# A convolution followed by a feed-forward layer on one core: GpSimd's additions one step later and spread out

## The chip, the core and the metric

The kernel runs on one core of a Trainium2 chip. The metric is the device time of one execution in microseconds (us). TensorE (PE in the profile) multiplies matrices, VectorE (DVE) and ScalarE (ACT) work element by element, GpSimd (POOL) does that too and issues some DMAs, and SyncE (SP) issues the other DMAs. PEld is the loading of a matmul's stationary operand, which overlaps with the matmul before it.

## The reference

The input x has 8 x 4096 tokens of 192 channels. First comes a causal convolution over 7 tokens, with weights that are shared by groups of 24 channels; then a feed-forward layer of width 2048 with a piecewise activation.

```python
w = softmax(weight, axis=-1)                      # 8 groups x 7 taps
y[t, c] = sum(w[c // 24, k] * x[t - 6 + k, c] for k in range(7))
h = y @ w_in                                      # 192 -> 2048
g = np.where(h >= 1, h, np.where(h <= -1, 0, (h + 1) ** 2 / 4))
out = g @ w_out                                   # 2048 -> 192
```

## The kernel before, in words

The 32768 tokens are worked through in 64 blocks of 512; two blocks make a chunk. A **step** q is one pair of 128-wide slices of the 2048 hidden units for one block, so a block has 8 steps, a chunk 16 (i = 0 to 15 in the code, blocks 0 to 7 and 8 to 15), and the kernel 512. Everything is written in one order by hand; each engine keeps that order.

float32 products are made from rounded parts: x is held as `hi` and `lo`, the activations as `gh` and `gl`. Of 192 channels, the first 128 stand in a "natural" and in a "swapped" copy (lower and upper 64 partitions exchanged), so that two 64-row matmuls run beside each other. One step on TensorE is 18 such pairs: `mm1(q)` (L475) takes the natural `hi, hi, lo`, the swapped `hi, hi, lo` and the remaining channels `rhi, rhi, rlo` in this order, then `mm2(q - 3)` (L528) nine pairs of gh, gl and of the sum of low parts, `m`.

In the code's step q ScalarE squares the activation of h(q) (L562, L563) and rounds g(q - 1) to `gh` (L573); VectorE makes `gl` (L579, `act_low(q - 1)`), their sum `m` over the two slices (L585, `act_sum(q - 1)`) and the activation's last part (L890, `act_most(q)`). h has two buffers in PSUM, so `mm1(q + 2)` waits for L890 of q. ScalarE starts on h(q) when `mm1(q)` is done; so what stands in the code's step i behind it runs while TensorE is in step i + 1. A **TensorE step** below counts by `mm1`.

Between this, the convolution of the next blocks is made: units `a` and `b` for the two blocks' natural channels, `r` for the remaining channels of both. `conv_slot(i, ...)` deals out its operations by tables (`PLAN_A`, `PLAN_B`, `PLAN_R`): "T" is a transpose on VectorE (L163), a number is a tap. Taps of `a` are made on VectorE (L232). Of `b` and `r`, ScalarE makes a product into a buffer `p` (L237), and GpSimd adds it to `y` or `r` (L129). "split" makes `hi` on ScalarE (L268) and `lo = y - hi` on GpSimd (L272), and SP issues two transfers of 64 partitions (L255, L256) that make the swapped copy of each. Unit `b` of a chunk has its transpose and first taps at i = 12, 14 and 15 of the chunk before, the others and its split (i = 5) in its own chunk; its block starts at i = 8. The split of `a` stands at i = 12, for a block that starts at i = 0 of the next chunk.

From chunk 2 on, additions are not issued at once but kept in `held`, and `add_held` issues them behind that step's `act_sum` (each waits for the sum `m` by a dependency named "port"). The subtraction for `lo` is not held. GpSimd also issues four adding DMAs for a block's output (L619).

Of the kernel before, what the change touches and what calls it, by code (L numbers as in the profile page):

```python
# [8 lines left out]
F32 = mybir.dt.float32  # L9
# [22 lines left out]
def lightconv_then_ffn(ctx: ExitStack, tc: tile.TileContext, x, weight, w_in, w_out, out):  # L32
# [24 lines left out]
    nc = tc.nc  # L57
# [63 lines left out]

    pending = []

    held = []

    def add_held(behind):

        for out, a, b in held:
            add = nc.gpsimd.tensor_add(out, a, b)  # L129
            if behind is not None:  # L130
                tc.add_manual_dep(add.ins, behind.ins.name, mybir.DependencyInfo(
                    mybir.DependencyClass.Sync, mybir.DependencyReason.DATA), reason="port")
        held.clear()

    def let_go():

# [10 lines left out]
    class Conv:  # L147
# [92 lines left out]
        def taps(self, *ks):  # L240
            y = self.y
            for k in ks:
                if k == 0:
                    nc.scalar.mul(y, self.xT[:, SH:SH + TB], wk[:, self.wsel, 0:1])  # L244
                elif self.c == 1 and self.u != "b":
                    pending.append((y, y, self.product(k)))
                elif self.c > 1:
                    held.append((y, y, self.product(k)))
                else:
                    nc.gpsimd.tensor_add(y, y, self.product(k))  # L250

# [4 lines left out]
            nc.sync.dma_start(out=w[BOT].bitcast(F32), in_=t[TOP].bitcast(F32))  # L256
            return w

        def split(self, eng=None):
            for _ in self.splits(eng or nc.gpsimd):  # L260
                pass

        def splits(self, eng):

            o = xop[2 * self.c + (self.u == "b")]
            hi = xo.tile([P, TB], F32R, name="hi0")
            lo = xo.tile([P, TB], F32R, name="lo0")
            nc.scalar.copy(hi, self.y)  # L268
            for key, t in (("hi", hi), ("lo", lo)):
                if key == "lo":  # L270
                    yield
                    eng.tensor_sub(lo, self.y, hi.bitcast(F32))  # L272
                w = self.swapped(t, key + "1", 3)
                o["n", key] = (t[TOP], t[BOT])
                o["s", key] = (w[TOP], w[BOT])
            yield

        def split_rest(self):

# [520 lines left out]
    def whole(j, *cols):  # L800
        for _ in chunks[j].bits(*cols):
# [25 lines left out]

    PLAN_B = {12: ("T",), 14: (0, 1), 15: (2, 3), 1: (4,), 2: (5,), 3: (6,), 5: "split"}  # L830
    PLAN_A = {1: ("T",), 2: (0,), 4: (1,), 6: (2,), 7: (3,), 9: (4,), 10: (5,), 11: (6,),
              12: "split"}
    PLAN_R = {2: ("T",), 4: (0,), 6: (1,), 7: (2,), 8: (3, 4), 9: (5,), 11: (6,), 13: "split"}
    SECOND_B = {0: (0, 1), 1: (2,), 2: (3,), 3: (4,), 4: (5, 6), 5: "split"}


# [5 lines left out]
    def conv_slot(i, b, a, r):  # L842
        early = b is not None and b.c == 0
        plans = ((None if early else b, SECOND_B if b and b.c == 1 else PLAN_B),
                 (a, FIRST_A if early else PLAN_A),
                 (r, FIRST_R if early else PLAN_R))
        for u, plan in plans:
# [119 lines left out]
    for q in range(NQ + LATE):  # L967
# [16 lines left out]
        done = q - (DELAY if q < NF32 + DELAY else LATE)  # L984
        if done < 0 or q == NF32 + DELAY:
            done = None
# [27 lines left out]
        else:  # L1014
# [17 lines left out]
            if q < NQ:  # L1032
                conv_slot(i, conv_b if i < 8 else conv_n.get("b"), conv_n.get("a"),
                          conv_n.get("r"))
            add_held(act_sum(n) if low else None)
            if q == NQ - 1:
                act_low(q - 1)
# [50 lines left out]
```

## Time and profile before

| what | value |
|---|---|
| median of 3 runs | 2046.57 us (2046.46 to 2049.79) |
| the profiled execution | 2046.76 us |
| its span in the profile | 2045.0 us |
| PE, DVE, ACT, POOL busy | 100%, 96%, 96%, 39% |

The span runs from the first to the last instruction of the profiled execution; 1.8 us of its time lie outside. A busy PE counts pipelined matmuls, so that short waits of its loads hardly show in the busy share.

### The profile page before, as it was taken

What the parts mean: (1) busy time and instruction counts of PE and PEld (TensorE: products, weight loads), DVE (VectorE), ACT (ScalarE), POOL (GpSimd) and SP (SyncE); (2) the same over time, 40 slices, a digit from 0 to 9 for tenths busy, and PEclk for the clock granted to TensorE, in tenths of its full rate; (3) what the DMA queues carried; (4) which work ended last, traced back from release to release, by engine and by line L of the source; (5) the groups of instructions that cost most, each with busy time, mean ns of one, the idle gap of its engine ahead of it and who ended that gap; (6) DMA issues with size and microseconds to landing.
All of it is one profiled execution on the core that took longest, in us unless ns stands there. A gap on an engine that the chain in (4) does not pass through costs nothing.

```text
span 2045.0 us, 46902 instructions
## 1 busy us (share of the span) xinstructions
PE 2037.9 (100%) x18644; PEld 1756.9 (86%) x18644; DVE 1966.2 (96%) x2109; ACT 1960.4 (96%) x2381; POOL 792.8 (39%) x749
## 2 busy tenths in 40 slices
PE   9999999999999999999999999999999999999999
PEld 6998888888888888888888888888888888888888
DVE  8899999999999999999999999999999999999998
ACT  8799999999999999999999999999999999999997
POOL 1544343343433443334434344343343333443431
PEclk9999999999999999999999999999999999999999
DMA  7333333443434434334333344343343433433323
GB/s 178 80 62 70 69 71 71 85 76 56 81 68 79 80 65 77 71 67 87 70 66 73 72 82 76 57 83 69 74 81 65 76 71 66 86 72 65 72 55 55
DMA packets 470685, 152.27 MB, mean 74 GB/s; under 512 B 418944, under 2 KB 426624, under 8 KB 470464
## 3 DMA queue, kind: packets, MB, share of 16 engines
q1 hardware_dynamic: 446880, 109.17, 25.4%
q0 software_dynamic: 23424, 39.99, 13.4%
q8 instruction: 146, 2.39, 0.5%
q14 instruction: 75, 0.61, 0.1%
q10 hardware_dynamic: 160, 0.10, 0.0%
HBM read 32.84 MB, written 25.17 MB: 28 GB/s over the span
## 4 chain that ended last, share of the span: by engine, by line
PE 68%; DVE 15%; ACT 13%; issue 4%; DVEq 0%; ACTq 0%; POOL 0%; POOLq 0%
PE h L475 35%; PE accr L528 20%; PE accm L528 10%; DVE gl L579 7%; DVE g L890 4%; ACT gh L573 3%; ACT g L562 3%; ACT g L563 3%; DVE m L585 3%; ACT p L237 3%; DVE osb L631 1%; PE accm L495 1%; PE accr L495 1%; ACT t L609 0%; ACT y L244 0%
## 5 line engine op out<-in xcount | busy, mean ns | idle before, releaser
L579 DVE TENSOR_TENSOR gl<-g,gh 128x1024 fp32r<-128x1024 f32 x495 | 728.1, 1471 | 23.4 <-ACT gh L573 17.1
L890 DVE SCALAR_TENSOR_TENSOR g<-g,h 128x1024 f32<-128x1024 f32 x504 | 607.5, 1206 | 4.8 <-ACT g L563 2.8
L475 PE MATMUL h<-hi,w 64*128 64x512 f32 x4032 | 609.4, 380 | 1.5
L528 PE MATMUL accr<-gh,wg 64*128 64x512 f32 x3960 | 590.1, 376 | 0.0
L562 ACT ACTIVATE g<-h 128x1024 f32<-128x1024 f32 (+1 forms) x497 | 507.2, 1020 | 41.6 <-PE h L475 39.9
L563 ACT ACTIVATE g<-g 128x1024 f32<-128x1024 f32 (+1 forms) x497 | 526.6, 1060 | 15.8
L573 ACT CAST gh<-g 128x1024 fp32r<-128x1024 f32 x495 | 514.4, 1039 | 0.5 <-DVE g L890 0.4
L129 POOL TENSOR_TENSOR y<-y,p 128x512 f32<-128x512 f32 x180 | 231.0, 1283 | 573.3 <-ACT p L237 300.5
L475 PEld LDWEIGHTS h<-hi,w 64*128 64x128 f32 x4032 | 376.0, 186 | 76.4 <-DVE g L890 28.2
L528 PEld LDWEIGHTS accr<-gh,wg 64*128 64x128 f32 x3960 | 373.9, 185 | 53.2
L129 POOL TENSOR_TENSOR r<-r,p 128x512 f32<-128x512 f32 x180 | 232.5, 1291 | 476.6 <-DVE m L585 420.0
L475 PE MATMUL h<-lo,w 64*128 64x512 f32 x2016 | 383.8, 376 | 0.0
L528 PE MATMUL accr<-gl,words 64*128 64x512 f32 x1980 | 376.3, 376 | 0.0
L585 DVE TENSOR_TENSOR m<-gl 128x512 fp32r<-128x512 f32 x495 | 348.0, 703 | 20.6 <-PE h L475 0.5
L528 PE MATMUL accm<-gh,wg 64*128 64x512 f32 x1980 | 295.1, 376 | 0.0
L475 PE MATMUL h<-rh,w 64*128 64x512 f32 x992 | 293.6, 376 | 0.0
L475 PE MATMUL h<-rhi,w 64*128 64x512 f32 x992 | 293.6, 376 | 0.0
L619 POOL DMA_DIRECT2D t<-t x244 | 206.0, 983 | 97.6 <-DMA t<-t 75.6
L475 PEld LDWEIGHTS h<-lo,w 64*128 64x128 f32 x2016 | 192.2, 186 | 25.9
L528 PEld LDWEIGHTS accr<-gl,words 64*128 64x128 f32 x1980 | 188.3, 186 | 26.0
L528 PEld LDWEIGHTS accm<-gh,wg 64*128 64x128 f32 x1980 | 188.0, 186 | 26.0
L475 PEld LDWEIGHTS h<-rhi,w 64*128 64x128 f32 x992 | 184.5, 186 | 12.9
(161 smaller groups left out, 2313.3 us busy)
## 6 DMA issues: line engine op xcount, KB each, us to landing
t<-t POOLq DMA_DIRECT2D x183, 128.0 KB, 4.1
out_dram<-osb SPq DMA_DIRECT2D x366, 64.0 KB, 1.9
raw<-in_x_dram SPq DMA_DIRECT2D x334, 68.0 KB, 2.6
hi<-hi SPq DMA_DIRECT2D x128, 128.0 KB, 3.4
lo<-lo SPq DMA_DIRECT2D x126, 128.0 KB, 3.1
t<-t POOLq DMA_DIRECT2D x61, 256.0 KB, 3.3
rhi<-rh SPq DMA_DIRECT2D x62, 128.0 KB, 4.1
rlo<-rl SPq DMA_DIRECT2D x62, 128.0 KB, 3.5
```

What stands on the lines that cost most here:

```text
L129: add = nc.gpsimd.tensor_add(out, a, b)
L237: nc.scalar.mul(p, self.xT[:, SH + k:SH + k + TB], wk[:, self.wsel, k:k + 1])
L475: nc.tensor.matmul(h[e], w[HALVES[e], c0:c0 + P], seen(x[e][e]), start=(n == 0), stop=(n == len(mms) - 1))
L495: nc.tensor.matmul(accs[s][a, i][:, c0:c0 + D], block, w[half, e, :], start=(j == 0 and e == 0 and b % 2 == 0), stop=(j == NPAIR - 1 and e ...
L528: mm = nc.tensor.matmul(accs[s][bank], w[half], in_turn(g[half]), start=(j == 0 and bank not in seen), stop=(j == NPAIR - 1 and k % 3 == 2 ...
L562: nc.scalar.activation(g[:, e, :], hs[q][:, e, :], AF.Relu, bias=0.5, scale=0.5)
L563: nc.scalar.activation(g[:, e, :], g[:, e, :], AF.Square)
L573: nc.scalar.copy(gh[:, e, :], gs[q][:, e, :])
L579: nc.vector.tensor_sub(gl[:, e, :], g[:, e, :], gh[:, e, :])
L585: return nc.vector.tensor_add(gt, gl[:, 0, :], gl[:, 1, :])
L619: nc.gpsimd.dma_start(out=to, in_=src, accum_op=ALU.add)
L890: nc.vector.scalar_tensor_tensor(out=g, in0=g, scalar=1.0, in1=h, op0=ALU.min, op1=ALU.max)
```

## The change: what it does

`held` now takes functions, and there is a second list, `fresh`. What `conv_slot` puts in goes to `fresh`; `add_held` issues what is in `held`, behind the step's `act_sum` as before, and then moves `fresh` to `held`. So each addition comes one step later than before. The subtraction for `lo` with its two transfers, of `a` and `b` from chunk 2 on, goes the same way: one step later, and behind the sum of low parts. Two table entries with two taps are spread (`b`: taps 2, 3 at i = 15 become 2 at 15 and 3 at 0; `r`: taps 3, 4 at i = 8 become 3 at 8 and 4 at 9).

```diff
-        for out, a, b in held:
-            add = nc.gpsimd.tensor_add(out, a, b)
+        for work in held:
+            done = work()
             if behind is not None:
-                tc.add_manual_dep(add.ins, behind.ins.name, mybir.DependencyInfo(
+                tc.add_manual_dep(done.ins, behind.ins.name, mybir.DependencyInfo(
                     mybir.DependencyClass.Sync, mybir.DependencyReason.DATA), reason="port")
-        held.clear()
+        held[:] = fresh
+        fresh.clear()
...
                 elif self.c > 1:
-                    held.append((y, y, self.product(k)))
+                    fresh.append(lambda p=self.product(k): nc.gpsimd.tensor_add(y, y, p))
...
-        def split(self, eng=None):
-            for _ in self.splits(eng or nc.gpsimd):
-                pass
+        def split(self):
+
+            if self.c < 2:
+                for _ in self.splits(nc.gpsimd):
+                    pass
+                return
+            parts = self.splits(nc.gpsimd)
+            next(parts)
+            fresh.append(lambda: next(parts))
...
                 if key == "lo":
                     yield
-                    eng.tensor_sub(lo, self.y, hi.bitcast(F32))
+                    sub = eng.tensor_sub(lo, self.y, hi.bitcast(F32))
...
-    PLAN_B = {12: ("T",), 14: (0, 1), 15: (2, 3), 1: (4,), 2: (5,), 3: (6,), 5: "split"}
+    PLAN_B = {12: ("T",), 14: (0, 1), 15: (2,), 0: (3,), 1: (4,), 2: (5,), 3: (6,), 5: "split"}
...
-    PLAN_R = {2: ("T",), 4: (0,), 6: (1,), 7: (2,), 8: (3, 4), 9: (5,), 11: (6,), 13: "split"}
+    PLAN_R = {2: ("T",), 4: (0,), 6: (1,), 7: (2,), 8: (3,), 9: (4,), 10: (5,), 11: (6,),
+              13: "split"}
```

On GpSimd, from the additions of unit `b` to its split and the first addition of `r`, with what each row waits for (DVE is the wait behind the sum, DMASW and DMAHW are transfers). Before:

```order
L129 TENSOR_TENSOR y<-y,p 128x512 [waits DVE_49,Activation_49,Pool_49] x3
L619 DMA t<-t 128x512 [waits DMASW3_49,DMASW2_49]
L619 DMA t<-t 64x512 [waits DMASW5_49]
L619 DMA t<-t 64x512 [waits DMASW4_49]
L619 DMA t<-t 64x512
L272 TENSOR_TENSOR lo_4261<-y,hi_4260 128x512 [waits DMAHW0_49,DMAHW1_49,PE_49,Activation_49]
L129 TENSOR_TENSOR r<-r,p 128x512 [waits DVE_49,Activation_49]
```

The same place in the changed kernel:

```order
L249 TENSOR_TENSOR y<-y,p 128x512 [waits DVE_49,Activation_49,Pool_49] x4
L627 DMA t<-t 128x512 [waits DMASW3_49,DMASW2_49]
L627 DMA t<-t 64x512 [waits DMASW5_49]
L249 TENSOR_TENSOR y<-y,p 128x512 [waits DVE_49,Activation_49,Pool_49]
L627 DMA t<-t 64x512 [waits DMASW4_49]
L627 DMA t<-t 64x512
L280 TENSOR_TENSOR lo_4261<-y,hi_4260 128x512 [waits DMAHW4_49,DMAHW5_49,DVE_49,Activation_49]
L249 TENSOR_TENSOR r<-r,p 128x512 [waits DVE_49,Activation_49]
```

The last addition of `b` now stands between the adding DMAs, and the subtraction waits for VectorE, where it waited for ScalarE (and for buffers) alone.

On SP's queue, the transfers for the splits of `a` (hi, lo) and `r` (rhi, rlo), between an output's store and the next. Before:

```order
L255 DMA hi_12162<-hi_12159 64x512
L256 DMA hi_12162<-hi_12159 64x512
L255 DMA lo_12166<-lo_12160 64x512
L256 DMA lo_12166<-lo_12160 64x512
L255 DMA rhi<-rh 64x512
L256 DMA rhi<-rh 64x512
L255 DMA rlo<-rl 64x512
L256 DMA rlo<-rl 64x512
```

After:

```order
L256 DMA hi_12161<-hi_12158 64x512
L257 DMA hi_12161<-hi_12158 64x512
L256 DMA rhi<-rh 64x512
L257 DMA rhi<-rh 64x512
L256 DMA rlo<-rl 64x512
L257 DMA rlo<-rl 64x512
L256 DMA lo_12229<-lo_12159 64x512
L257 DMA lo_12229<-lo_12159 64x512
```

The low part of `a` now leaves behind the four transfers of `r`. The transfers of unit `b` keep their place in the queue (hi, hi, lo, lo, then a store). TensorE's and VectorE's order is the same in both kernels.

## Rows read from the trace of the kernel before

**Rows 1.** The page: busy time of each engine, and groups of instructions.

```profile
PE 2037.9 (100%) x18644; PEld 1756.9 (86%) x18644; DVE 1966.2 (96%) x2109; ACT 1960.4 (96%) x2381; POOL 792.8 (39%) x749
L129 POOL TENSOR_TENSOR y<-y,p 128x512 f32<-128x512 f32 x180 | 231.0, 1283 | 573.3 <-ACT p L237 300.5
```

**Rows 2.** Waits of TensorE's loads, 270 to 2030 us: in total, times, longest.

```profile
PEld h L475 <- DVE g L890: 26.1, 77, 0.5
PEld accm L528 <- DVE m L585: 8.3, 21, 0.6
```

**Rows 3.** TensorE's order of time, first matmuls of some steps: start, us, what.

```profile
146.65 0.38 PE L475 MATMUL h<-hi,w 64*128 64x512 f32 x2
...
976.03 0.38 PE L475 MATMUL h<-hi,w 64*128 64x512 f32 x2
...
1003.22 0.38 PE L475 MATMUL h<-hi,w 64*128 64x512 f32 x2
...
2029.91 0.40 PE L475 MATMUL h<-hi,w 64*128 64x512 f32 x2
```

**Rows 4.** Busy time from chunk 2 on: us, PE, PEld, DVE, ACT, POOL, granted clock, DMA.

```profile
146.60:2029.90 1883.30, 1880.49 (x17246) 1622.02 (x17246) 1824.89 (x1879) 1826.88 (x2177) 737.24 (x675) 1.00 0.39 72
```

**Rows 5.** GpSimd's order of time at two additions, at one, and at a subtraction.

```profile
965.46 2.65 POOL L129 TENSOR_TENSOR y<-y,p 128x512 f32<-128x512 f32 x2 [2.33 <-ACT p L237]
...
1006.00 1.29 POOL L129 TENSOR_TENSOR r<-r,p 128x512 f32<-128x512 f32 x1 [2.52 <-DVE m L585]
...
953.03 1.40 POOL L272 TENSOR_TENSOR lo<-y,hi 128x512 fp32r<-128x512 f32 x1
```

**Rows 6.** VectorE's order of time beside them, and undisturbed.

```profile
966.91 2.28 DVE L579 TENSOR_TENSOR gl<-g,gh 128x1024 fp32r<-128x1024 f32 x1 [0.17 <-ACT gh L573]
...
971.90 1.22 DVE L579 TENSOR_TENSOR gl<-g,gh 128x1024 fp32r<-128x1024 f32 x1
...
1006.88 1.49 DVE L579 TENSOR_TENSOR gl<-g,gh 128x1024 fp32r<-128x1024 f32 x1
...
953.12 1.87 DVE L585 TENSOR_TENSOR m<-gl 128x512 fp32r<-128x512 f32 x1
```

**Rows 7.** GpSimd, 982 to 995 us: steps 4 to 7 of chunk 15.

```profile
982.65 1.29 POOL L129 TENSOR_TENSOR y<-y,p 128x512 f32<-128x512 f32 x1 [2.28 <-ACT p L237]
...
989.61 1.27 POOL L272 TENSOR_TENSOR lo<-y,hi 128x512 fp32r<-128x512 f32 x1 [0.56 <-ACT hi L268]
993.38 1.28 POOL L129 TENSOR_TENSOR r<-r,p 128x512 f32<-128x512 f32 x1 [2.49 <-DVE m L585]
```

**Rows 8.** VectorE, 985 to 994 us.

```profile
985.61 0.68 DVE L585 TENSOR_TENSOR m<-gl 128x512 fp32r<-128x512 f32 x1
...
987.34 1.21 DVE L579 TENSOR_TENSOR gl<-g,gh 128x1024 fp32r<-128x1024 f32 x1
...
990.50 1.46 DVE L579 TENSOR_TENSOR gl<-g,gh 128x1024 fp32r<-128x1024 f32 x1
...
992.55 0.68 DVE L585 TENSOR_TENSOR m<-gl 128x512 fp32r<-128x512 f32 x1
```

**Rows 9.** SP's queue after that subtraction.

```profile
991.05 1.22 SPq L255 DMA_DIRECT2D lo<-lo  x1
992.32 0.60 SPq L256 DMA_DIRECT2D lo<-lo  x1
```

**Rows 10.** The second transfer of `lo` behind the subtraction at 953 us.

```profile
L256 SPq DMA_DIRECT2D lo<-lo x1: 602/602/602, 955.0 to 955.0; - x1
...
DMA to landing us min/median/max: 2.6/2.6/2.6
```

**Rows 11.** The transfers of `lo` in all chunks, from issue to landing.

```profile
DMA to landing us min/median/max: 2.2/3.1/4.2
```

**Rows 12.** TensorE's loads at the start of step 8 of chunk 15.

```profile
995.24 0.41 PEld L475 LDWEIGHTS h<-hi,w 64*128 64x128 f32 x4
...
996.32 0.19 PEld L475 LDWEIGHTS h<-lo,w 64*128 64x128 f32 x2
```

More of the change, by code (lines that the diff above doesn't have):

```diff
@@ L122, in lightconv_then_ffn @@
     pending = []
-    held = []
+    held, fresh = [], []
     def add_held(behind):
-        for out, a, b in held:
-            add = nc.gpsimd.tensor_add(out, a, b)
+        for work in held:
+            done = work()
             if behind is not None:
-                tc.add_manual_dep(add.ins, behind.ins.name, mybir.DependencyInfo(
+                tc.add_manual_dep(done.ins, behind.ins.name, mybir.DependencyInfo(
                     mybir.DependencyClass.Sync, mybir.DependencyReason.DATA), reason="port")
-        held.clear()
+        held[:] = fresh
+        fresh.clear()
     def let_go():
@@ L268, in splits @@
             nc.scalar.copy(hi, self.y)
+            sub = None
             for key, t in (("hi", hi), ("lo", lo)):
@@ L275, in splits @@
                 o["s", key] = (w[TOP], w[BOT])
-            yield
+            yield sub
         def split_rest(self):
```

## The prediction

> **What bounds the kernel now.** I read the page first. TensorE, VectorE and ScalarE are all busy for 96 to 100% of the span and GpSimd for 39% [rows 1]; that names no bound, since three engines share it. So I asked what TensorE, whose work nobody can shorten here, waits for: from 270 us on its loads wait for VectorE and for nothing else, for L890 (which frees a PSUM buffer of h) and for the sum m [rows 2]. Then I measured how much time that is, by the distance between steps, not by the waits: a load is issued ahead of its matmul, so part of a load's wait costs nothing. Steps 3 to 10 of chunk 15 have no wait: 27.19 us for seven steps, 3.885 each [rows 3]. From the first step of chunk 2 (146.65 us) to the last of all (2029.91 us) there are 17246 / 36 = 479 steps [rows 4] in 1883.26 us [rows 3]; undisturbed, they take 479 x 3.885 = 1861. **About 22 us, 1.1% of the span, is all that any relief of VectorE can give.** The granted clock is 1.00 in that stretch [rows 4].
>
> Where VectorE loses time, its order of time shows. L579 reads two tensors from SBUF and takes 1.22 us undisturbed. Beside two additions of GpSimd that end at 965.46 + 2.65 = 968.11 it takes 2.28 and ends 1.08 later, at 969.19; beside one that ends at 1007.29 it takes 1.49 and ends at 1008.37, 1.08 later too [rows 5, 6]. The sum L585 at 953.12 us lasts 1.87 us beside the subtraction, which ends at 954.43, 0.56 before it [rows 5, 6]. So a VectorE instruction of this kind gets on only when GpSimd's has ended. An addition behind the sum m, with L890 between, costs L579 about 0.27 us; two in one step cost it 1.06; a subtraction at the wrong moment costs as much.
>
> **The change part by part.**
>
> *The spread taps and "at most one a step"* take the doubled additions from two of sixteen steps. For 1.06 us there is 0.27 in each of two steps, and a burst that made L890 late is gone. *The held subtraction* no longer meets L585. Each of these acts on the 22 us and on nothing else. I take 21 of it as won: 13 additions and subtractions of 0.27 us are left in a chunk, 3.5 us of 16 x 3.885 = 62.2, and VectorE's busy share was 1824.9 of 1883.3 us with the worse collisions in it [rows 4]. Bounds: 0 if the waits stay where they are, 22 if all go.
>
> *The additions one step later.* For `r` and `a`, what reads them comes a step or more behind; the last addition of `b` (tap 6, i = 3) now runs at i = 4, and its rounding stands at i = 5. The product buffers hold three; with one product a step the third next product comes after the addition. I cost this at nothing; its cover is one step (3.9 us) less one addition (1.3 us) [rows 5].
>
> *The subtraction of `b`, one step later.* This is what decides. It stood at i = 5 and ran in TensorE's step 6, as soon as ScalarE had rounded: 989.61 us in chunk 15 [rows 7]. Now it is issued at i = 6 behind the sum of that step. In the trace of before, the row of that very place is the first addition of `r` in step 7, at 993.38 us, 0.15 behind the sum that ends at 992.55 + 0.68 = 993.23 [rows 7, 8]. The block starts at i = 8. There TensorE's first loads are at 995.24 and the load for the swapped low part, the sixth of eighteen pairs, is at 996.32 [rows 12]. Between the end of the subtraction and this load lie two transfers on SP's queue. So the working in chunk 15:
>
> - When the sum ends in step 7. Before, L579 at 990.50 us was held by the subtraction (1.46 us [rows 8]); that goes, 0.25 earlier. But the last addition of `b`, at 982.65 in step 4 [rows 7], is followed now by another in step 5, behind the sum that ends at 986.29; it would end at 986.29 + 0.15 + 1.29 = 987.73 and hold the L579 of 987.34 to 988.81, where it ended at 988.55 [rows 8]: up to 0.26 later. The two cancel: 993.2.
> - Subtraction: starts at 993.35, 1.28 us as the addition in its place [rows 7]: 994.63.
> - Transfers: at 954.43 us a subtraction ended, the second issue came at 955.0 and landed 2.6 later [rows 10], 3.2 in all. In chunk 15 the first issue came 0.17 behind the end and the second 1.27 behind the first [rows 7, 9], so with the shortest landing of all, 2.2 [rows 11], it was 3.6. The median landing of 3.1 [rows 11] with the issues of rows 10 gives 3.7. I take 3.3, nearer to rows 10, since the transfers of `hi`, which were in flight just before those of rows 9, will by then have had a step more to land: 997.93.
> - TensorE's load stands from 996.32 to 997.93: **1.6 us**, and 0.1 that I add for taking up again (an estimate; bounds 0 and 0.2). Nothing hides it: mm1 is one accumulation in a fixed order, and all that follows on TensorE is queued behind it: mm2 of three steps back, the next mm1, then ScalarE and VectorE that wait for h.
>
> Bounds of the wait: with 2.2 for the landing and a sum as early as 992.8, 0.7; with 4.2 for the landing and rows 9's issues, 3.1. It comes once in each of the chunks 2 to 31, 30 times: 30 x 1.7 = 51 us. The longer wait also gives VectorE slack, so that the 21 us are won the more surely.
>
> [...]
>
> *The subtraction of `a`*, at i = 13 now, has three steps to the start of its block where that of `b` has two. By the same working it lands 3.9 - 1.6 = 2.3 us ahead of its load, less what VectorE runs later there and less the wait behind the four transfers of `r`, some 1 us (an estimate). Cost nothing; without that cover its lateness would come on top, 30 us for each us.
>
> **Sum.** The profiled execution took 2046.76 us, 0.2 above the median of 2046.57. 2046.6 - 21 + 51 = 2076.6; I say **2076**.
>
> **The rivals.**
>
> 1. *The transfer is hidden or the release comes earlier: faster.* If the subtraction hung on the sum of the step before, it would end 3.9 us earlier than I read the code, at 990.7, and land at 994.0, ahead of the load. Then only the gain is left: 2046.6 - 21 = 2026. For it: the change may be read so that "one step later" counts from the additions' own sum. Against it: the first addition of `r` comes from the list in the same way, and in the order of instructions the subtraction now stands right before it with the same wait for VectorE. It decides from where the low part lands before 996.32, 1.6 us earlier than worked out. Chance 0.10.
> 2. *Gain and loss cancel.* A wait of 0.70 us a chunk gives back just the 21 us: 2047 (2042 to 2052). It needs the shortest landing and an earlier sum at once. Chance 0.07.
> 3. *It stands longer.* Landings of 4.2 us, VectorE late in step 7 in part of the chunks, or the low part of `a` late as well: 3.2 us x 30 = 96, 2122; with one of these in half the chunks about 2099. Chance 0.12.
> 4. *The 22 us do not go*, since 13 single holds remain: 2046.6 + 51 = 2098, at the upper end of the likeliest. No chance of its own.
>
> The likeliest, slower by the wait of `b`, has 0.71 and its own range of 2056 to 2098 (waits of 1.0 to 2.4 us with 21 us won).
>
> **How the numbers follow.** The likeliest's 0.71 does not reach 0.8, so the range takes in the upper edge of rival 2 and the lower part of rival 3: 2051 to 2101. A measurement of this kernel tells about 0.2% (4 us) from no change. Faster by more: rival 1 and a small part of 2, 0.12. Within: the middle of 2, 0.03. Slower: the rest, 0.85.
>
> **What would show it.** The profile after should list a new wait of TensorE's loads at mm1's line for a DMA of `lo`, some 30 times and 1 to 2 us each, the longest of all its waits, in step 8 of each chunk; L579 beside GpSimd at no more than 1.5 us; the waits for L890 and m nearly gone; the subtraction of `b` 0.15 us behind the sum m, where its row now names ScalarE. If the wait for `lo` is absent or under 0.7 us, the step on the deadline is wrong; if it is there and the time is still lower, the 22 us were undercounted. If the waits for L890 remain, the step on the collisions is wrong.

## The result and the profile after

The changed kernel takes 2065.9 us (median of 6 runs, 2065.24 to 2066.58), the one before 2046.67 us (6 runs, 2046.15 to 2049.79): a ratio of 1.0091, 95% interval 1.0078 to 1.0104. It is slower by 0.9%; the forecast was 2076, in a range of 2051 to 2101. The profiled execution took 2066.58 us, its span is 2064.9.

The page of the changed kernel: busy times, the chain of work that ended last by engine, and two groups of instructions.

```profile
PE 2055.8 (100%) x18644; PEld 1860.3 (90%) x18644; DVE 1882.4 (91%) x2109; ACT 1962.2 (95%) x2381; POOL 783.6 (38%) x749
...
PE 66%; ACT 14%; DVE 10%; issue 4%; DMA 4%; POOL 2%; SPq 1%; ACTq 0%; DVEq 0%; POOLq 0%
...
L587 DVE TENSOR_TENSOR gl<-g,gh 128x1024 fp32r<-128x1024 f32 x495 | 651.3, 1316 | 118.2 <-ACT gh L581 113.5
...
L249 POOL TENSOR_TENSOR y<-y,p 128x512 f32<-128x512 f32 x180 | 231.4, 1285 | 524.0 <-ACT p L238 214.4
```

VectorE is busy for 84 us less than before [rows 1]; the execution is 20 us longer all the same. GpSimd's additions last as long as before. In the chain a DMA, GpSimd and SP's queue now have shares (none of the three had 1% before), and L587 (L579 before) waits 113 us for ScalarE's cast, where it waited 17. TensorE's own waits, in total, times and longest, from 270 us to the end:

```profile
PEld h L483 <- DMA lo<-lo: 24.0, 57, 0.6
PEld h L483 <- DVE g L899: 11.2, 28, 0.4
PEld accm L536 <- DVE m L593: 9.2, 27, 0.3
```

Against [rows 2] the first line is new, and each of the two waits for VectorE now comes about once a chunk. How much time the waits cost is again taken from the distance of steps. TensorE's first matmuls of chunk 2, of steps 8, 9, 14, 15 of chunk 15 and of the step behind it, and of the last step:

```profile
147.35 0.38 PE L483 MATMUL h<-hi,w 64*128 64x512 f32 x2
...
1005.16 0.38 PE L483 MATMUL h<-hi,w 64*128 64x512 f32 x2
...
1009.83 0.38 PE L483 MATMUL h<-hi,w 64*128 64x512 f32 x1
...
1029.26 0.38 PE L483 MATMUL h<-hi,w 64*128 64x512 f32 x1
...
1033.62 0.48 PE L483 MATMUL h<-hi,w 64*128 64x512 f32 x2
...
1037.61 0.38 PE L483 MATMUL h<-hi,w 64*128 64x512 f32 x2
...
2049.76 0.40 PE L483 MATMUL h<-hi,w 64*128 64x512 f32 x2
```

The 479 steps from chunk 2 on take 1902.41 us, 41.5 more than 479 x 3.885 = 1860.9; before it was 22.3 [rows 3]. The difference of 19 us is the result. Step 8 of chunk 15 takes 4.67 us (0.785 lost), steps 14 and 15 take 4.36 and 3.99 (0.58 lost together). The same subtraction for every step of chunks 2 to 31, for this kernel and those of the experiments below, summed by the place in the chunk (us lost; steps 3 to 7 lose nothing in any of them). The kernel before, run beside them, took 2047.02 us (e1 to e4), 2046.2 (e5 to e8) and 2044.0 (e9, e10):

| kernel | all | step 0 | 1, 2 | 8 | 9 to 13 | 14, 15 | median, us |
|---|---|---|---|---|---|---|---|
| before | 22.3 | 0 | 9.5 | 0.1 | 11.8 | 1.0 | 2046.67 |
| changed | 41.5 | 1.6 | 0 | 23.1 | 0.1 | 16.7 | 2065.9 |
| e1: b's low part at once | 15.6 | 0.7 | 0 | 0 | 0 | 14.9 | 2040.93 |
| e2: old table of r | 25.8 | 0.2 | 0 | 25.7 | 0 | 0 | 2050.77 |
| e3: e1 and e2 | 2.0 | 1.0 | 0 | 0 | 1.0 | 0 | 2027.2 |
| e4: tables alone | 15.0 | 0 | 0 | 0 | 6.6 | 8.3 | 2039.82 |
| e5: e1, r's taps early | 1.5 | 0.7 | 0 | 0.2 | 0.6 | 0 | 2025.91 |
| e6: a's low part at once | 62.2 | 0 | 0 | 22.5 | 0.1 | 39.6 | 2088.39 |
| e7: late additions alone | 28.5 | 0 | 0 | 0 | 0.1 | 28.4 | 2054.16 |
| e8: b's low part late alone | 35.3 | 0 | 11.8 | 22.8 | 0.8 | 0 | 2059.8 |
| e9: swapped low part last | 21.5 | 0 | 0 | 4.5 | 0.3 | 16.7 | 2045.9 |

So the 22 us of before are gone (steps 1, 2, 9 to 13 lose next to nothing), and 41 us of new waits stand in their place, at two points of the chunk (in 29 of the 30 chunks) and in four chunks at a third, step 0.

**Step 8.** The changed kernel's sum of step 7 on VectorE, the subtraction on GpSimd, the transfers on SP's queue, and TensorE's loads, in chunk 15:

```profile
1002.02 0.68 DVE L593 TENSOR_TENSOR m<-gl 128x512 fp32r<-128x512 f32 x1
```

```profile
1002.84 1.28 POOL L280 TENSOR_TENSOR lo<-y,hi 128x512 fp32r<-128x512 f32 x1 [4.09 <-ACT p L238]
```

```profile
1004.15 0.46 SPq L256 DMA_DIRECT2D lo<-lo  x1
1004.66 0.60 SPq L257 DMA_DIRECT2D lo<-lo  x1
...
DMA to landing us min/median/max: 2.2/2.3/2.3
```

```profile
1005.60 0.41 PEld L483 LDWEIGHTS h<-hi,w 64*128 64x128 f32 x4
1006.40 0.18 PEld L483 LDWEIGHTS h<-lo,w 64*128 64x128 f32 x1 [0.39 <-DMA lo<-lo]
1007.03 0.18 PEld L483 LDWEIGHTS h<-lo,w 64*128 64x128 f32 x1 [0.45 <-DMA lo<-lo]
```

The subtraction follows the sum (1002.70) by 0.14 us and ends at 1004.12. The second transfer is issued 0.54 us later and lands 2.3 us after that: 2.9 us from the end of the subtraction to the landing. The second half of the swapped copy is loaded at 1007.03 instead of 0.87 us into the step, 1006.03. GpSimd's wait is put down to a product of ScalarE that had long been done; that the subtraction starts 0.14 us behind the sum in every chunk shows that it was the sum.

**Steps 14 and 15.** ScalarE's order of time around its four copies of an output, in chunk 15 of the changed kernel:

```profile
1017.99 1.05 ACT L617 COPY t<-accr 128x512 f32<-128x512 f32 x2
1018.93 1.08 ACT L617 COPY t<-accm 128x512 f32<-128x512 f32 x2
1019.88 0.75 ACT L238 ACTIVATE p<-r,wk 128x512 f32<-128x512 f32 x1
1020.50 1.06 ACT L581 CAST gh<-g 128x1024 fp32r<-128x1024 f32 x1
```

And VectorE behind it:

```profile
1018.24 1.21 DVE L899 SCALAR_TENSOR_TENSOR g<-g,h 128x1024 f32<-128x1024 f32 x1
1021.60 1.22 DVE L587 TENSOR_TENSOR gl<-g,gh 128x1024 fp32r<-128x1024 f32 x1 [2.16 <-ACT gh L581]
...
1031.14 0.69 DVE L291 TENSOR_TENSOR rl<-r,rh 128x512 fp32r<-128x512 f32 x1 [0.74 <-ACT rh L290]
1031.75 0.68 DVE L593 TENSOR_TENSOR m<-gl 128x512 fp32r<-128x512 f32 x1
1032.35 1.21 DVE L899 SCALAR_TENSOR_TENSOR g<-g,h 128x1024 f32<-128x1024 f32 x1
```

A product of r now stands between the copies and the cast (tap 5, which the new table puts at i = 10). In the kernel before the cast came right behind the copies:

```profile
1008.33 1.09 ACT L609 COPY t<-accm 128x512 f32<-128x512 f32 x2
1009.28 1.08 ACT L573 CAST gh<-g 128x1024 fp32r<-128x1024 f32 x1
```

VectorE stands idle for 2.16 us in front of L587. ScalarE has no idle time in these steps, so it is still late when it rounds r, which VectorE's L291 waits for. That rounding, in the changed kernel and in e2 below, where r's table is the old one:

```profile
1030.51 0.60 ACT L290 CAST rh<-r 128x512 fp32r<-128x512 f32 x1
```

```profile
1022.32 0.60 ACT L290 CAST rh<-r 128x512 fp32r<-128x512 f32 x1
```

From the start of step 10 (1013.72 and 1006.14 us) that is 16.79 and 16.18 us: 0.6 late. The wait for `rh` alone does not tell it, for e2 has such a wait too (0.85 us) and loses nothing. The sum and L899 follow late, L899 ends at 1033.56, and the next mm1 starts at 1033.62.

### The profile page after: what moved, and what is told of

It reads as the page before. It is cut to its first block, busy times and chain, and to the rows that moved or that the text cites. A ratio compares the mean times of both kernels' runs of the same rounds, so it can differ in the third digit from the quotient of the medians.

```text
span 2064.9 us, 46868 instructions
## 1 busy us (share of the span) xinstructions
PE 2055.8 (100%) x18644; PEld 1860.3 (90%) x18644; DVE 1882.4 (91%) x2109; ACT 1962.2 (95%) x2381; POOL 783.6 (38%) x749
## 3 DMA queue, kind: packets, MB, share of 16 engines
q1 hardware_dynamic: 446880, 109.17, 25.7%
## 4 chain that ended last, share of the span: by engine, by line
PE 66%; ACT 14%; DVE 10%; issue 4%; DMA 4%; POOL 2%; SPq 1%; ACTq 0%; DVEq 0%; POOLq 0%
PE h L483 33%; PE accr L536 20%; PE accm L536 10%; DVE gl L587 6%; ACT gh L581 4%; DMA lo<-lo 4%; ACT p L238 3%; ACT g L570 3%; ACT t L617 2%; DVE g L899 2%; POOL lo L280 2%; DVE y L233 1%; DVE m L593 1%; PE accm L503 1%; PE accr L503 1%
## 5 line engine op out<-in xcount | busy, mean ns | idle before, releaser
L587 DVE TENSOR_TENSOR gl<-g,gh 128x1024 fp32r<-128x1024 f32 x495 | 651.3, 1316 | 118.2 <-ACT gh L581 113.5
L536 PE MATMUL accr<-gh,wg 64*128 64x512 f32 x3960 | 643.4, 377 | 0.0
L899 DVE SCALAR_TENSOR_TENSOR g<-g,h 128x1024 f32<-128x1024 f32 x504 | 608.0, 1206 | 4.9 <-ACT g L571 2.8
L483 PEld LDWEIGHTS h<-hi,w 64*128 64x128 f32 x4032 | 436.5, 186 | 41.3 <-DVE g L899 12.5
L483 PE MATMUL h<-lo,w 64*128 64x512 f32 x2016 | 450.8, 379 | 4.8 <-DMA lo<-lo 1.6
L536 PEld LDWEIGHTS accr<-gh,wg 64*128 64x128 f32 x3960 | 412.7, 185 | 35.9
L536 PE MATMUL accr<-gl,words 64*128 64x512 f32 x1980 | 426.1, 376 | 0.0
L483 PEld LDWEIGHTS h<-lo,w 64*128 64x128 f32 x2016 | 244.5, 186 | 40.3 <-DMA lo<-lo 26.1
L536 PEld LDWEIGHTS accr<-gl,words 64*128 64x128 f32 x1980 | 237.1, 186 | 14.9
L536 PEld LDWEIGHTS accm<-gh,wg 64*128 64x128 f32 x1980 | 220.6, 186 | 15.1
L536 PE MATMUL accm<-m,words 64*128 64x512 f32 x990 | 216.5, 382 | 0.0
```

The lines of the kernel that those rows point to most:

```text
L483: nc.tensor.matmul(h[e], w[HALVES[e], c0:c0 + P], seen(x[e][e]), start=(n == 0), stop=(n == len(mms) - 1))
L536: mm = nc.tensor.matmul(accs[s][bank], w[half], in_turn(g[half]), start=(j == 0 and bank not in seen), stop=(j == NPAIR - 1 and k % 3 == 2 ...
L587: nc.vector.tensor_sub(gl[:, e, :], g[:, e, :], gh[:, e, :])
L899: nc.vector.scalar_tensor_tensor(out=g, in0=g, scalar=1.0, in1=h, op0=ALU.min, op1=ALU.max)
```

## The experiments

Two theories are tested. Theory 1: step 8 loses time because the low part of b lands behind its load. Theory 2: steps 14 and 15 lose time because a product of r now stands at i = 10, between ScalarE's copies and its cast.

**e1.** In the changed kernel, only unit b's low part is subtracted at once again.

```diff
-            if self.c < 2:
+            if self.c < 2 or self.u == "b":
```

> Only the split of unit b is taken out of the change: its low part is subtracted at once, as before; everything else stays as changed. Theory 1 (the low part of b misses its place in mm1 of step 8): the 0.78 us that step 8 loses in each of 29 chunks go, 22.7 us, so 2066 becomes about 2043; the loads' wait for a DMA of lo stays only in the few chunks where it is that of a. Rival (the loss sits in the additions that come later, and step 8 only shows it): within 4 us of 2066.

Measured: 2040.93 us, a ratio of 0.9968 to before (0.9957 to 0.9980). Step 8 loses nothing, and TensorE's waits from 270 us on are:

```profile
PEld h L483 <- DVE g L899: 10.9, 27, 0.4
PEld accm L536 <- DVE m L593: 9.7, 27, 0.4
PEld h L483 <- DMA lo<-lo: 0.6, 2, 0.3
```

The waits for VectorE are those of steps 14 and 15, as in the changed kernel. Theory 1 holds, the rival falls; with this one line put back the change makes the kernel faster, by 0.3%.

**e2.** In the changed kernel, only the table of r is that of before.

```diff
-    PLAN_R = {2: ("T",), 4: (0,), 6: (1,), 7: (2,), 8: (3,), 9: (4,), 10: (5,), 11: (6,),
-              13: "split"}
+    PLAN_R = {2: ("T",), 4: (0,), 6: (1,), 7: (2,), 8: (3, 4), 9: (5,), 11: (6,), 13: "split"}
```

> Only the table of r goes back to that of before (taps 3 and 4 at i = 8, none at i = 10); everything else stays as changed. Theory 2 (the product that now stands at i = 10, behind four copies on ScalarE, makes the cast to gh 0.6 us late, VectorE stands idle in step 11 and is late in step 14): the 0.57 us that steps 14 and 15 lose in each of 30 chunks go, 17 us, so 2066 becomes about 2049, and VectorE's wait for the cast falls from 113 us to under 60. Rival (the additions and subtractions that now hold VectorE in steps 12 to 14 do it): steps 14 and 15 go on losing 0.5 us or more, and the time stays within 5 us of 2066.

Measured: 2050.77 us, ratio 1.0019 (1.0010 to 1.0028). Steps 14 and 15 lose nothing; of TensorE's waits that for lo is the only one left from 270 us to the end of the steps:

```profile
PEld h L483 <- DMA lo<-lo: 22.8, 54, 0.6
```

VectorE's wait for the cast fell from 113.5 us, a little less than expected:

```profile
DVE gl L587 <- ACT gh L581: 62.5, 94, 2.3
```

Theory 2 holds. The doubled addition of r, one step later, costs nothing here.

**e3.** Both edits together.

> The split of b at once and the old table of r together; the additions stay one step later behind the sum, the table of b stays spread, the low part of a stays held. By theories 1 and 2 both losses go: 2066 - 22.7 - 17 = about 2026, and 2024 if the few waits for the low part of a go as well. If the wait in step 8 had given VectorE the slack that hid the doubled addition of r, new waits for L890's line come back in steps 9 to 11, 0.3 us in 30 chunks: about 2036. Rival (the later additions cost the time): 2046 or more.

Measured: 2027.2 us, ratio 0.9904 (0.9889 to 0.9919). 2.0 us are lost in all; the two losses add up, and steps 9 to 13, with the doubled addition of r, lose 1 us in all, not 10.

**e4.** The kernel before with the two new tables and nothing else of the change.

> The kernel before with the two spread tables alone: additions in their own step, low parts at once. Of its 22 us of waits, the 9.5 us of steps 1 and 2 should go by the spread of b. The spread of r puts a product at i = 10: by theory 2 VectorE is late in step 14 here too, 0.4 to 0.6 us in 30 chunks, 12 to 17 us: so about 2046 + 15 - 9.5 = 2050 (2040 to 2056), with waits of steps 14 and 15 in all chunks. Rival (the later additions make the wait of steps 14 and 15): these steps lose nothing and the time is 2026 to 2032.

Measured: 2039.82 us, ratio 0.9966 (0.9953 to 0.9979), 0.2 us below what theory 2 gave. Steps 1 and 2 lose nothing: the spread of b alone removes the 9.5 us. Steps 14 and 15 lose time without any later addition, but only 0.28 us a chunk, where I had expected 0.4 to 0.6; another 0.2 us are lost in steps 12 and 13. That the product at i = 10 makes these last ones too is likely, but no run shows it. The collisions of before that cost steps 9 to 11 are gone too.

**e5.** As e1, with a table of r that has one tap a step and none beside the copies.

```diff
-    PLAN_R = {2: ("T",), 4: (0,), 6: (1,), 7: (2,), 8: (3,), 9: (4,), 10: (5,), 11: (6,),
+    PLAN_R = {2: ("T",), 4: (0,), 5: (1,), 6: (2,), 7: (3,), 8: (4,), 9: (5,), 11: (6,),
               13: "split"}
```

> The changed kernel with the split of b at once and a table of r that has one tap a step and none at i = 10 (taps 1 to 6 at i = 5, 6, 7, 8, 9, 11). Theory 2 (a product behind ScalarE's four copies is what makes steps 14 and 15 wait): no such wait, about 2025 to 2029 as with the old table. If it is the spread of r as such (one addition a step, up to i = 11, that holds VectorE) the waits of steps 14 and 15 come back: 2041 as with the split of b at once alone. A product more on ScalarE at i = 5 may make the cast of step 6 late: up to 0.3 us a chunk, 2035.

Measured: 2025.91 us, ratio 0.9902 (0.9887 to 0.9917). The additions are as spread as in the change and steps 14 and 15 lose nothing, so it is the place beside the copies that costs, not the spread. ScalarE goes from the copies to the cast, as before:

```profile
999.96 1.08 ACT L617 COPY t<-accm 128x512 f32<-128x512 f32 x2
1000.91 1.08 ACT L581 CAST gh<-g 128x1024 fp32r<-128x1024 f32 x1
```

With e3 this is the fastest kernel here; its 479 steps take 1.5 us more than undisturbed ones.

**e6.** In the changed kernel, a's low part is subtracted at once (the line of e1 with "a").

> The changed kernel with the low part of a subtracted at once; that of b stays held. The 0.3 to 0.45 us that step 0 loses in 4 chunks should go (1.6 us). In step 13 the subtraction now stands ahead of r's last addition, which it pushes behind its own end: two holds of VectorE in one step, as with doubled additions, and VectorE is late there already: by the theory of the exclusive hold steps 13 to 15 lose 0.5 to 1.1 us more in 30 chunks: 2080 to 2097. Rival (the held subtraction in step 14 is itself what makes L890's successor late in step 14): 0.57 us a chunk go, about 2048.

Measured: 2088.39 us, ratio 1.0208 (1.0193 to 1.0223). The time is in the expected range, and the waits of step 0 are gone, but the mechanism is another than I wrote. GpSimd and VectorE in step 13 of chunk 15:

```profile
1038.16 1.28 POOL L280 TENSOR_TENSOR lo<-y,hi 128x512 fp32r<-128x512 f32 x1 [0.52 <-ACT hi L275]
1039.42 2.27 POOL L249 TENSOR_TENSOR r<-r,p 128x512 f32<-128x512 f32 x1
```

```profile
1039.35 1.21 DVE L587 TENSOR_TENSOR gl<-g,gh 128x1024 fp32r<-128x1024 f32 x1
1042.38 0.69 DVE L291 TENSOR_TENSOR rl<-r,rh 128x512 fp32r<-128x512 f32 x1 [1.82 <-ACT rh L290]
```

L587 does not suffer: it started 0.07 us ahead of the addition, and now it is the addition that is held and takes 2.27 us instead of 1.28. What needs it, the rounding of r, is late, and VectorE stands idle for 1.82 us, where it was 0.74 in the changed kernel. So the hold goes both ways.

**e7.** Only the additions are one step later: tables of before, both low parts at once.

> The part of the change that delays the additions by one step, alone: tables of before, low parts at once as before. By theories 1 and 2 this part costs nothing by itself: neither the wait for lo in step 8 nor that of steps 14 and 15 appears, and the doubled additions only move one step on: 2030 to 2050. Rival (the later additions cost time): 2055 or more.

Measured: 2054.16 us, ratio 1.0041 (1.0026 to 1.0056). A miss: neither wait that I named appears, and steps 1, 2 and 9 to 13 lose nothing, but 14 and 15 lose 28.4 us. GpSimd's and VectorE's rows in step 13 of chunk 15 show the place that e6 showed:

```profile
1023.23 2.29 POOL L249 TENSOR_TENSOR r<-r,p 128x512 f32<-128x512 f32 x1
```

```profile
1023.18 1.21 DVE L587 TENSOR_TENSOR gl<-g,gh 128x1024 fp32r<-128x1024 f32 x1
1026.20 0.69 DVE L291 TENSOR_TENSOR rl<-r,rh 128x512 fp32r<-128x512 f32 x1 [1.82 <-ACT rh L290]
```

The last addition of r, one step later, comes behind a's low part, starts 0.05 us behind L587's start and ends at 1025.52, 1.13 us behind L587's end. Holding a's low part back, as the change does, takes the addition out of this place.

**e8.** The kernel before with b's low part one step later behind the sum, nothing else.

> The kernel before with one thing changed: the low part of b is subtracted one step later, behind the sum. Theory 1: step 8 waits for lo in 30 chunks, 1.0 to 1.3 us each, since VectorE is later in step 7 here than in the changed kernel: 30 to 39 us on 2047. The wait gives VectorE slack, so that the waits of before in steps 9 to 14 (12.9 us) go, while those of steps 1 and 2 (9.5 us) stay: 2064 to 2073. Rival (no net loss, the slack gives all back): 2047 to 2052.

Measured: 2059.8 us, ratio 1.0069 (1.0052 to 1.0086): slower, but less than the expected 2064. Step 8 loses 0.76 us a chunk, about as in the changed kernel, not 1.0 to 1.3, since the sum of step 7 ends as early (2.46 us ahead of step 8 in both). The waits of steps 1 and 2 stay (11.8 us), those of 9 to 14 go but for 0.8 us.

**e9.** In the changed kernel, the swapped low part is the last of mm1's nine pairs.

```diff
+            mms.append(mms.pop(5))
```

> The changed kernel with another order of mm1: the swapped low part's pair stands last of the nine instead of sixth, three pairs (0.65 us) later; GpSimd, VectorE and ScalarE are left as changed. Theory 1 (the loss of step 8 is the load that comes before its data): step 8 loses 0.65 us less in 29 chunks, 0.1 to 0.2 instead of 0.78, and the waits of step 0 in 4 chunks go: 2066 - 19 - 1.6 = about 2045. Rival (the transfers or the subtraction disturb TensorE or VectorE by themselves): within 4 us of 2066.

Measured: 2045.9 us, ratio 1.0011 (1.0001 to 1.0020) to the 2044.0 of the kernel before. Step 8 loses 0.15 us instead of 0.78. GpSimd's and SP's work was left as it was, so the loss comes from the load that stands before its data, and not from the transfers or the subtraction as such. TensorE's waits:

```profile
PEld h L484 <- DMA lo<-lo: 5.0, 27, 0.3
```

**e10.** In the changed kernel, b's low part is held one step more.

```diff
-            if behind is not None:
+            if behind is not None and done is not None:
...
-            fresh.append(lambda: next(parts))
+            if self.u == "b":
+                fresh.append(lambda: fresh.append(lambda: next(parts)))
+            else:
+                fresh.append(lambda: next(parts))
```

> The changed kernel with the low part of b held one step more, so that it is subtracted in TensorE's step 8, behind r's first two additions. Theory 1: the subtraction ends about 2.7 us into step 8 and the swapped copy lands 2.7 us later, 5.4, where the load stands 0.87 into the step: a wait of 4.5 us instead of 0.78, 3.7 more in 29 or 30 chunks: 2066 + 110 = about 2176 (2160 to 2190), with the granted clock still 1.00. If so long a stand lowered the clock, more than 2200 and a granted clock under 1. Rival (other work fills the wait): under 2120.

Measured: 2273.65 us, ratio 1.1125 (1.1106 to 1.1143), with a mean granted clock of 0.956. The direction is theory 1's, the size is not: this is the case named in the expectation in which so long a stand lowers the clock. TensorE's loads in step 8 of a chunk, and the busy times by stretch (PE, PEld, DVE, ACT, POOL, then the granted clock, DMA share and GB/s):

```profile
1099.88 0.28 PEld L486 LDWEIGHTS h<-lo,w 64*128 64x128 f32 x2 [3.61 <-POOL lo L283]
...
1102.11 0.28 PEld L486 LDWEIGHTS h<-lo,w 64*128 64x128 f32 x1 [1.30 <-DMA lo<-lo]
```

```profile
1095.00:1096.50 1.50, 1.50 (x16) 1.13 (x12) 1.50 (x2) 1.47 (x2) 0.00 (x0) 1.00 0.00 0
1096.50:1100.00 3.50, 0.29 (x4) 0.12 (x2) 3.50 (x5) 1.72 (x3) 2.50 (x2) 0.84 0.00 0
1100.00:1102.00 2.00, 1.53 (x6) 0.72 (x6) 1.86 (x3) 0.00 (x0) 0.12 (x1) 0.50 0.48 111
...
1105.00:1106.00 1.00, 1.00 (x8) 0.82 (x6) 0.00 (x0) 0.97 (x2) 0.00 (x0) 0.66 0.82 131
1106.00:1107.00 1.00, 1.00 (x12) 0.96 (x10) 0.01 (x1) 1.00 (x2) 0.00 (x0) 1.00 0.75 118
```

The natural low part, too, is late here, which I had left out, and stops the loads for 3.61 us; the granted clock falls from 1.00 to 0.50, from 2.4 to 1.2 GHz, before that stand is over at 1099.88 us, and is back at 1.00 between 1105 and 1106 us, while TensorE works. In 29 of the 30 chunks step 8 loses 7.0 to 8.1 us, where a wait of 4.5 was expected. How much of it is the natural part and how much the clock, no run separates.

## Why the prediction was right, and where it was not

*What can be won.* About 22 us, all relief of VectorE: right. In the changed kernel these waits are gone, and e3 and e5 lose only 2.0 and 1.5 us in all. More than one part of the change wins them: the tables alone clear steps 1, 2 and 9 to 11 (e4), the later additions alone steps 1, 2 and 9 to 13 (e7), so the runs do not share the 22 us out among the parts. That a VectorE instruction with two SBUF inputs ends 1.08 us behind GpSimd's also held. In step 13 of chunk 15 of the changed kernel:

```profile
1024.26 1.29 POOL L249 TENSOR_TENSOR r<-r,p 128x512 f32<-128x512 f32 x1 [4.50 <-ACT p L238]
```

```profile
1025.16 1.47 DVE L587 TENSOR_TENSOR gl<-g,gh 128x1024 fp32r<-128x1024 f32 x1
```

From 270 us on no L587 took more than 1.50 us, so single additions cost it 0.28 us at most. It was half of the rule: the other half (e6, e7) holds GpSimd.

*The subtraction of b.* The step that decided, and it was right: place, cause and cost on the path (e1, e8, e9). Its size was off: the term was 1.7 us a chunk and measured 0.78. The sum ended 1.42 us into step 7, not 1.63: I let the new addition of step 5 delay it by what the missing hold gave, but that delay was taken up in step 6, where L587 waited for ScalarE's cast anyway (e8 shows the same 1.42). The transfers took 2.9 us, not 3.3: landings were 2.3 us with nothing else in flight. Nothing had to be added for taking up again. And "nothing hides it" was wrong by 0.2 us: the load came 1.0 us late, but it stands that much ahead of its matmul (0.87 us into the step, the sixth of 18 pairs of matmuls 5/18 of 3.885, 1.08), and the step lost 0.785. 0.2 + 0.4 + 0.1 + 0.2 is the difference; 30 x 1.7 = 51 us became 23, in 29 chunks, for the last one loses nothing. The sign to look for came accordingly: not one wait of 1 to 2 us a chunk, but two of at most 0.6. The upper bound of 3.1 us, from which the third rival's 3.2 comes, goes with the issues of rows 10; with those of rows 9, as it is written, it is 4.0. It did not come into play.

*The spread taps.* Here a step failed. I wrote that each of these edits "acts on the 22 us and on nothing else", weighed the spread on VectorE and GpSimd, and not on the engine that makes the products. The new place at i = 10 is the step in which ScalarE copies an output, and it costs 16.7 us in steps 14 and 15 (e2, e5, and in a weaker form e4). The profile of before had ScalarE at 96%, and its order showed the cast right behind the copies. So the waits for L899 and `m` did not go, by which the prediction would have called its step on the collisions wrong; but with r's old table they are gone (e2), so they are not those of the collisions. The sum's 13 additions and subtractions a chunk are 14, twelve and two, which changes nothing.

*The subtraction of a.* Costed at nothing, with about 1 us of cover: nearly right. In four chunks step 0 lost 0.34 to 0.44 us, 1.6 us in all; the second transfer of the low part landed 4.2 to 4.4 us behind its issue there, behind r's four transfers on SP's queue.

*The additions one step later.* Costed at nothing: right within the change, not by itself: e7 loses 28 us in steps 14 and 15 where the held subtraction of a is missing.

So 2076 came out near 2066 by luck, from two errors of opposite sign: 28 us too much for the one wait, 17 us not seen. Without the unseen 17 the time is that of e2, 2050.77 us, just below the range. Of the rivals, the one on the other side (a release a step earlier) did not happen. That gain and loss cancel would have needed a loss of 0.70 us a chunk, and step 8 lost 0.78, close to it: without the product at i = 10 the change is near even (e2).

## What to carry to other kernels

When work is moved a step later to clear one engine, follow it to its last reader, with the transfers between, and set the landing against that reader's load; here 0.8 us lost at one load of each chunk ate all that clearing VectorE had won, and putting that one item back (e1) kept the gain. When a table is spread, look up what the new place holds on every engine that the item uses: the free place for GpSimd was a step that four copies already filled on ScalarE. And measure what a bound's waits cost as the distance of steps over their undisturbed length: the sum over the places in a chunk shows where to look, and an experiment then which edit it belongs to.

## What the runs showed of the hardware that I had not expected

The exclusion between VectorE and GpSimd works in both directions: an addition that started 0.05 us behind L587's start took 2.29 us instead of 1.28 and ended 1.13 us behind L587's end (e7). The Trainium skill's page "SBUF — State Buffer", section "SBUF: two separate sides", says that whichever starts first keeps the shared ports for its whole instruction; the rows agree.

TensorE's clock fell to 1.2 GHz (a granted clock of 0.50) in e10 while its loads stood for 3.61 us, and came back to 1.00 while it worked. In the changed kernel, whose loads stand 0.39 and 0.45 us in such a step 8, the granted clock is 1.00 from chunk 2 to the last step.
